# A cross network on one core: the residual's first tile turned by halves, a half store cut into two quarters around the last turn, and four sums done one by one

## The chip, the cores and the metric

The kernel runs on one core of one Trainium2 chip. The metric is the device time of one execution in microseconds (us); the medians and ranges below are over several runs. A profiled execution gives the rows that are quoted: start and duration of each instruction on TensorE (PE, and PEld for its weight loads), VectorE (DVE), ScalarE (ACT), GpSimd (POOL), and of the DMA issues on SyncE's and ScalarE's queues (SPq, ACTq).

## The reference

The input has B = 16384 rows of D = 416 features in bf16. Six layers follow, each with a 416 x 416 weight:

```python
x = x0
for l in range(L):                       # L = 6
    proj = jnp.einsum('bd,de->be', x, ws[l]) + bs[l]
    x = x0 * proj + x
return x                                 # (16384, 416), bf16
```

So each layer is a matmul, a bias, a product with the input and a sum with the layer's own input (the residual).

## The kernel before

**Tiles and jobs.** The rows are cut into eight groups of 2048, and a job (g, l) is layer l of group g. Inside a job everything is turned: features lie on the partitions, rows along the free axis, in four chunks of 512 rows (j = 0 to 3). The 416 features are three full tiles of 128 (i, or t, = 0 to 2) and a remainder of 32, whose four chunks are packed into one tile of 128 partitions (the "tail"). The 48 jobs run in the order of the list `order`, in which several groups are under way at once so that no job waits for the one before it. The last jobs are (7,4), (6,5) and (7,5): the eighth group is group 7, the seventh is group 6.

**From a chunk to the next layer.** For a tile of a job, TensorE adds up the products of a chunk in a PSUM bank. ScalarE evacuates it with the bias (line 567), VectorE multiplies two chunks at a time with x0 (line 579) and adds the job's input (line 584), which gives the next layer's x. From the job (0,2) on, TensorE's order is the string `ORDER`, which `replay` turns into a list of matmuls of 32 rows each; the function `evacuate_chunk` is called when a chunk is done, and after the sum of two chunks (a "half" of the tile) it calls what depends on it.

**Queues.** `add` appends an instruction to the queue of its engine, in program order, and notes what it reads and writes. `_solve` puts in the waits. All instructions of one engine's queue go in that order, so what is added to SP behind a waiting DMA waits too. A DMA belongs to a lane, a semaphore of its own. Within a lane, the DMAs of one batch wait until the batch before has landed; a batch is named by the argument of that name. At the end SP waits for every lane whose name starts with "out" (lines 163 and 181).

**The output of a group.** x is turned back by DMA transposes into `ost`, which has rows on the partitions, and stored. For group 6 this goes by halves: `half_done` issues the turn of a half tile as soon as its sum is there (line 921). After the turn of the second half of tile 1 it issues the store of the first half of the group's rows, 832 KB (`store(g, 0, 2)`, line 946). The halves of job (6,5) come in the order (0, first), (1, first), (2, first), (0, second), (1, second), (2, second), so the turn of the last one is the only turn behind that store. The remainder goes through `turn_rest` (line 916), its copy into `ost` through POOL (line 939). The store of the second half stands later in the program, behind the first tile store of group 7.

**The last job.** (7,5) is done the other way round: with the x as weights, so that the result has rows on the partitions and needs no turn. Its 2048 rows are four tiles kk of 512 rows, each in four parts j of 128 rows. For that, its residual has to be turned: `x5n`, in the space of the x0 of slot 5. `rest_turn` (line 958) does that by DMA for the tiles 0 and 1, and TensorE for tile 2 and the tail. Tile 0 is turned whole when it is finished, tile 1 by halves when it is finished. A memset on POOL (line 956), which writes the same tokens, stands for "the old x0 has been read". For each kk, ScalarE copies out the four parts (line 1206), VectorE multiplies them with x0 (`nat_mul`, line 1212) and adds the residual (`nat_add`, line 1218), and a store takes them out (`nat_store`, line 1225). For kk = 0 to 2 this goes in pairs of j, and one store takes all four (416 KB). For kk = 3 the products are single; the sums of j = 0 and 1 are one instruction, with one store of 208 KB, and those of j = 2 and 3 are single, with stores of 104 KB each, the first on SP, the second on ACT.

Of the kernel before, what the change touches and what calls it, by code (L numbers as in the profile page):

```python
# [3 lines left out]
P = 128  # L4
CH = 512
# [16 lines left out]
class Program:  # L22
# [12 lines left out]
    def add(self, eng, fn, reads=(), writes=(), lane=None, batch=None, hold=False, release=False, row=None):  # L35
        op = Op(eng, fn, lane, batch, row)
        deps = {}
        if eng == "pool":
            writes = list(writes) + ["pool"]
        for t in reads:  # L40
            w = self.writer.get(t)
            if w is not None:
                deps[id(w)] = (w, True)
        for t in writes:
            w = self.writer.get(t)
            if w is not None:
                deps[id(w)] = (w, True)
            for r in self.readers.get(t, ()):
                if id(r) not in deps:
                    deps[id(r)] = (r, False)  # L50
        for d, raw in deps.values():
            if d.lane is None and d.eng == eng and lane is None and (eng == "pe" or not raw):
                if row is None or d.row is None or row == d.row:
                    continue
            op.deps.append(d)
        for t in reads:
            self.readers.setdefault(t, []).append(op)
        for t in writes:
            self.writer[t] = op
            self.readers[t] = []  # L60
        if eng == "dve":
            if hold:
                self.flush()
                self.held = op
            else:
                self.queue[eng].append(op)
                if release:
                    self.flush()
        else:
            self.queue[eng].append(op)  # L70
        if lane is not None:
            batches = self.lanes.setdefault(lane, [])
            if not batches or batches[-1][0] != batch:
                batches.append((batch, []))
            batches[-1][1].append(op)
        return op
# [230 lines left out]
def bass_standalone__cross_network_dcn__recsys_kernel(  # L307
# [7 lines left out]
    L = ws.shape[0]  # L315
    NT = 3
    NJ = 4
    GC = NJ * CH
    NG = B // GC
    KK = CH // P  # L320
    assert D == NT * P + T32 and B == NG * GC and NG == 8 and L == 6
    LAST = NG - 1
# [26 lines left out]
    xs = [nc.alloc_sbuf_tensor(f"x_{s}", [P, XW], BF16) for s in range(NXS)]  # L349
# [205 lines left out]
    def evacuate_chunk(g, l, i, j, b, read):  # L555

        s0 = slot(g)
        if (g, l, i) not in tile_tw:
            tile_tw[(g, l, i)] = tw_n[0] % NTW
            tw_n[0] += 1  # L560
            tile_out[(g, l, i)] = set()
        r, out_ = tile_tw[(g, l, i)], tile_out[(g, l, i)]
        if (g, l + 1) not in xset:
            xset[(g, l + 1)] = free_x.pop(0)
        src, stok = x_src(g, l)
        so = xset[(g, l + 1)]
        add("act", lambda h: h.activation(  # L567
            tw[r][:, j * CH:(j + 1) * CH], bank(b), ACT_F.Identity, bias=bias[:, i, l:l + 1], scale=1.0),
            reads=[("ps", b), "bias"], writes=[("tw", r, j)])
        out_.add(j)  # L570
        a = j - j % 2
        ready[(g, l, i, a)] = max(ready.get((g, l, i, a), 0), read)
        if not {a, a + 1} <= out_:
            return
        both = (a, a + 1)
        o, c = slice(a * CH, (a + 2) * CH), slice(i * GC + a * CH, i * GC + (a + 2) * CH)

        def multiply():
            add("dve", lambda h: h.tensor_tensor(tw[r][:, o], tw[r][:, o], x0s[s0][:, c], ALU.mult),  # L579
                reads=[("tw", r, k) for k in both] + [x0_tok(s0, i, k) for k in both],  # L580
                writes=[("tw", r, k) for k in both], release=True)

        def plus():
            add("dve", lambda h: h.tensor_tensor(xs[so][:, c], tw[r][:, o], src(i, a, a + 2), ALU.add),  # L584
                reads=[("tw", r, k) for k in both] + [stok(i, k) for k in both],
                writes=[("x", so, i, k) for k in both], hold=True)
            if len(out_) == NJ or (g, l) in halved and i == NT - 1:
                pr.flush()

        todo = [multiply, plus]  # L590
        if (g, l) in halved:
            todo.append(lambda: half_done(g, l, i, a))
        if len(out_) == NJ:
            todo.append(lambda: finish_tile(g, l, 1, i))
        while todo:
            if behind_tail or phases and max(dve[0], ready[(g, l, i, a)]) + PAIR > phases[0] + 14:
                behind_tail.extend(todo)
                return
            step = todo.pop(0)
            if step in (multiply, plus):  # L600
                dve[0] = max(dve[0], ready[(g, l, i, a)]) + PAIR
            step()
# [316 lines left out]
    def turn_out(g, t, j0, j1):  # L919
        s = xset[(g, L)]  # L920
        add("sp", lambda h: h.dma_start_transpose(
            ost[:, j0 * KK:j1 * KK, t * P:(t + 1) * P], xs[s][:, t * GC + j0 * CH:t * GC + j1 * CH]),
            reads=[("x", s, t, j) for j in range(j0, j1)], writes=[("ost", t, j) for j in range(j0, j1)],
            lane=f"ot_{t}{j0}", batch=g)

    def half_done(g, l, i, a):
        turn_out(g, i, a, a + 2)
        if (i, a) == (NT - 2, 2):
            store(g, 0, 2)

    def spread(eng):

# [8 lines left out]
    def store(g, j0, j1):  # L941

        rows = out[g * GC + j0 * CH:g * GC + j1 * CH, :]
        o = ost[:, j0 * KK:j1 * KK, :].rearrange("p (j k) f -> p j k f", k=KK)
        pat = "(j p k) f -> p j k f" if g == 0 else "(j k p) f -> p j k f"
        add("sp", lambda h: h.dma_start(rows.rearrange(pat, j=j1 - j0, k=KK), o),
            reads=[("ost", t, j) for t in range(NT + 1) for j in range(j0, j1)],
            writes=[("out", g, j0)], lane="out", batch=(g, j0))

    x5f = x0s[s5][:, 0:XW + CH].rearrange("p (a f) -> p a f", f=D)  # L950

    def rest_turn(t):

        s = xset[(LAST, L - 1)]
        if t == 0:
            add("pool", lambda h: h.memset(warm[:, :], 0.0), writes=x0_all(s5) + x03_toks(s5) + ["x5 free"])
        for j0, j1 in ((0, NJ),) if t == 0 else ((0, 2), (2, NJ)):
            add("sp", lambda h, j0=j0, j1=j1: h.dma_start_transpose(
                x5f[:, j0 * KK:j1 * KK, t * P:(t + 1) * P], xs[s][:, t * GC + j0 * CH:t * GC + j1 * CH]),
                reads=[("x", s, t, j) for j in range(j0, j1)] + ["x5 free"],  # L960
                writes=[("x5n", j, t) for j in range(j0, j1)], lane=f"x5_{t}{j0}", batch=0)

    items = []
    where = {(b[0 if b in batches[4:-3] else min(1, len(b) - 1)], 0): b for b in batches[:-1]}
# [43 lines left out]
    def finish_tile(g, l, n=1, i=0):  # L1008
        tiles_done[(g, l)] = tiles_done.get((g, l), 0) + n
        if l == L - 1 and g == LAST - 2:  # L1010
            turn_out(g, i, 0, NJ)
        elif (g, l) == (LAST, L - 2) and i < NT - 1:
            rest_turn(i)
        elif (g, l, i) == (LAST - 1, L - 2, 0):
            spread("dve")
            store(LAST - 2, 0, NJ)
        if tiles_done[(g, l)] == NT:
            done_with(g, l)
# [190 lines left out]
    def nat_mul(kk, j, n=2):  # L1209
        o, x0v = on[:, j:j + n, kk, :], x0n7[:, j:j + n, kk, :]  # L1210
        toks = [("on", a, kk) for a in range(j, j + n)]
        add("dve", lambda h: h.tensor_tensor(o, o, x0v, ALU.mult),  # L1212
            reads=toks + [("n7", k) for k in range(KK)], writes=toks)

    def nat_add(kk, j, n=2):
        o, x5v = on[:, j:j + n, kk, :], x5n[:, j:j + n, kk, :]
        toks = [("on", a, kk) for a in range(j, j + n)]
        add("dve", lambda h: h.tensor_tensor(o, o, x5v, ALU.add),  # L1218
            reads=toks + [("x5n", a, t) for a in range(j, j + n) for t in range(NT + 1)], writes=toks)
# [33 lines left out]
    for kk in range(1, KK):  # L1253
        begun = (1,) if kk == 1 else ()
        nat_rows(kk, bks[kk], begun=begun)
        for j in range(NJ):
            nat_full(kk, j, bks[kk][j], False, (2,) if j in begun else range(NT))
            nat_out(kk, j, bks[kk])
            if kk == last:
                nat_mul(kk, j, 1)  # L1260
            elif j % 2:
                nat_mul(kk, j - 1)
                nat_add(kk, j - 1)
            if kk == last and j == 1:
                nat_add(kk, 0)
                nat_store(kk, 0, 2)
        if kk < last:
            nat_store(kk, 0, NJ)
# [33 lines left out]
```

## Time and profile before

| | |
|---|---|
| median of 3 runs | 466.54 us |
| lowest and highest | 466.38 and 467.29 us |
| profiled execution | 466.98 us |
| its span | 465.2 us |
| mean granted TensorE clock | 0.999 |
| busy: PE, DVE, ACT, POOL | 458.9, 403.3, 381.9, 7.2 us |
| moved by DMA | 53.78 MB, 116 GB/s in the mean |

The span runs from the first to the last instruction of the execution; the profiled execution's own time is 1.78 us longer. A row of the time line has the start, the duration, the engine or queue, the line of the kernel, the operation, what is written from what, the shape and the count. For a DMA on SPq or ACTq the duration is that of its issue by the queue, not of the transfer. A row of busy shares by stretch has the stretch and its length, then the busy time (and count) of PE, PEld, DVE, ACT and POOL, and last the granted clock, the mean busy share of the 16 DMA engines and what they moved in GB/s; the share can be a little over 1, since packets overlap.

### The profile page before, as it was taken

The page shows a single profiled execution, that of the slowest core. Times are in us where ns is not written, and L with a number is a line of the kernel's source. Part 1 is how long each engine was busy: PE and PEld are TensorE (multiplying, and loading weights), DVE is VectorE, ACT ScalarE, POOL GpSimd, SP SyncE. Part 2 cuts the span into 40 slices and gives each one's busy share as a digit, 9 for nine tenths or more (in the row PEclk, how much of TensorE's full clock was granted, in tenths as well). Part 3 has the DMA queues.
Part 4 walks back from the last instruction along what each step waited for, and adds up shares of the span by engine and source line. Part 5 has one row for each costly group of instructions (what it writes and reads, how often), then busy time and mean ns, then how long its engine had stood idle before and what let it go on. Part 6 is the DMA issues. An engine that isn't in the chain of part 4 may idle for free.

```text
span 465.2 us, 17826 instructions
## 1 busy us (share of the span) xinstructions
PE 458.9 (99%) x8001; PEld 267.2 (57%) x8001; DVE 403.3 (87%) x696; ACT 381.9 (82%) x609; POOL 7.2 (2%) x15
## 2 busy tenths in 40 slices
PE   9999999999999999999999999999999999999995
PEld 5444656575655556565665556566556665556552
DVE  1887888988889898898988979898988988989996
ACT  4686889887988889797888889888888887988884
POOL 1000000000000000000000000000000000000000
PEclk9999999999999999999999999999999999999999
DMA  8985759000002849086469616677100088182898
GB/s 228 188 174 127 166 118 195 13 23 9 19 4 36 157 163 194 14 133 179 91 136 130 182 29 92 96 121 216 26 2 4 25 148 296 38 137 65 200 162 291
DMA packets 136720, 53.78 MB, mean 116 GB/s; under 512 B 113210, under 2 KB 135236, under 8 KB 136644
## 3 DMA queue, kind: packets, MB, share of 16 engines
q1 hardware_dynamic: 136488, 52.54, 52.4%
q8 instruction: 62, 1.02, 0.9%
q10 hardware_dynamic: 156, 0.11, 0.1%
q14 instruction: 14, 0.11, 0.1%
HBM read 5.97 MB, written 13.63 MB: 42 GB/s over the span
## 4 chain that ended last, share of the span: by engine, by line
PE 94%; DVE 2%; DMA 1%; ACT 1%; SPq 1%; issue 0%; DVEq 0%
PE ps L1092 73%; PE ps L708 7%; PE ps L1096 6%; PE ps L661 4%; PE ps L655 1%; PE ps L696 1%; DMA x<-in_x_dram 1%; DVE x L1218 1%; DVE x L1212 1%; ACT tw L567 1%; PE ps L682 1%; SPq L751 0%; DVE tw L579 0%; DVE x L584 0%; PE ps L806 0%
## 5 line engine op out<-in xcount | busy, mean ns | idle before, releaser
L1092 PE MATMUL ps<-x,wm 32*128 32x512 bf16 x6288 | 372.8, 375 | 0.0
L567 ACT ACTIVATE tw<-ps,bias 128x512 bf16<-128x512 f32 x524 | 326.9, 688 | 48.8 <-PE ps L1092 35.9
L1092 PEld LDWEIGHTS ps<-x,wm 32*128 32x128 bf16 x6288 | 222.6, 92 | 134.7 <-ACT tw L567 6.4
L579 DVE TENSOR_TENSOR tw<-tw,x 128x1024 bf16<-128x1024 bf16 x262 | 177.1, 690 | 41.0 <-ACT tw L567 39.6
L584 DVE TENSOR_TENSOR x<-tw,x 128x1024 bf16<-128x1024 bf16 x262 | 171.2, 689 | 0.3
L1096 PE MATMUL ps<-x,w 32*128 32x512 bf16 x524 | 159.7, 375 | 0.0
L1096 PEld LDWEIGHTS ps<-x,w 32*128 32x128 bf16 x524 | 44.6, 92 | 5.9
L708 PE MATMUL ps<-x,wm 128*32 128x512 bf16 x564 | 33.6, 380 | 0.0
L628 ACT ACTIVATE ts<-ps,bias 128x512 bf16<-128x512 f32 x32 | 20.4, 685 | 13.1 <-PE ps L696 13.1
L531 ACT ACTIVATE tw<-ps,bias 128x1024 bf16<-128x1024 f32 (+1 forms) x24 | 20.7, 937 | 8.2 <-PE ps L682 7.0
L708 PEld LDWEIGHTS ps<-x,wm 128*32 128x32 bf16 x564 | 13.5, 96 | 18.2 <-ACT tw L567 3.7
L661 PE MATMUL ps<-x,wm 128*128 128x512 bf16 x92 | 21.6, 384 | 0.0
L632 DVE TENSOR_TENSOR x<-ts,x 128x512 bf16<-128x512 bf16 x47 | 18.4, 420 | 0.3
L661 PEld LDWEIGHTS ps<-x,wm 128*128 128x128 bf16 x92 | 8.5, 98 | 11.5 <-issue 2.3
L540 DVE TENSOR_TENSOR tw<-tw,x 128x1024 bf16<-128x1024 bf16 (+1 forms) x21 | 13.1, 637 | 2.2 <-ACT tw L531 2.1
L624 DVE SCALAR_TENSOR_TENSOR ts<-ps,bias,x 128x512 bf16<-128x512 f32 x15 | 11.2, 747 | 3.1 <-PE ps L696 3.1
L545 DVE TENSOR_TENSOR x<-tw,x 128x1024 bf16<-128x1024 bf16 (+1 forms) x21 | 12.6, 635 | 0.0
L630 DVE TENSOR_TENSOR ts<-ts,x 128x512 bf16<-128x512 bf16 x32 | 12.4, 418 | 0.0
L939 POOL COPY ost<-ot 128x512 bf16<-128x512 bf16 x6 | 5.8, 964 | 390.4 <-DMA ot<-x 390.4
L816 DVE COPY x<-ps 128x512 bf16<-128x512 bf16 x5 | 2.0, 423 | 8.7 <-PE ps L806 8.7
L1157 PE MATMUL ps<-wm,x 128*128 128x416 bf16 x48 | 9.3, 340 | 0.0
L1206 ACT ACTIVATE x<-ps 128x416 bf16<-128x416 f32 x16 | 7.7, 528 | 1.5 <-PE ps L1157 1.5
(51 smaller groups left out, 72.9 us busy)
## 6 DMA issues: line engine op xcount, KB each, us to landing
out_dram<-ost SPq DMA_DIRECT2D x6, 1664.0 KB, 7.7
x<-x SPq DMA_DIRECT2D x24, 96.0 KB, 2.2
x<-in_x_dram SPq DMA_DIRECT2D x8, 208.0 KB, 3.9
x<-in_x_dram SPq DMA_DIRECT2D x4, 416.0 KB, 8.0
out_dram<-ost SPq DMA_DIRECT2D x2, 832.0 KB, 4.2
wm<-in_ws_dram SPq DMA_DIRECT2D x5, 312.0 KB, 3.4
x<-x SPq DMA_DIRECT2D x22, 64.0 KB, 2.0
out_dram<-x SPq DMA_DIRECT2D x3, 416.0 KB, 4.5
```

The costliest lines, as they stand in the source:

```text
L531: add("act", lambda h, a=a, w=w, b0=b0: h.activation(tw[r][:, a * CH:(a + w) * CH], psum[:, b0 * CH:(b0 + w) * CH], ACT_F.Identity, bias=b ...
L540: add("dve", lambda h, a=a, e=e: h.tensor_tensor(tw[r][:, a * CH:e * CH], tw[r][:, a * CH:e * CH], x0s[s0][:, i * GC + a * CH:i * GC + e * ...
L545: add("dve", lambda h, a=a, e=e: h.tensor_tensor(xs[so][:, i * GC + a * CH:i * GC + e * CH], tw[r][:, a * CH:e * CH], src(i, a, e), ALU.ad ...
L567: add("act", lambda h: h.activation(tw[r][:, j * CH:(j + 1) * CH], bank(b), ACT_F.Identity, bias=bias[:, i, l:l + 1], scale=1.0), reads=[( ...
L579: add("dve", lambda h: h.tensor_tensor(tw[r][:, o], tw[r][:, o], x0s[s0][:, c], ALU.mult), reads=[("tw", r, k) for k in both] + [x0_tok(s0 ...
L584: add("dve", lambda h: h.tensor_tensor(xs[so][:, c], tw[r][:, o], src(i, a, a + 2), ALU.add), reads=[("tw", r, k) for k in both] + [stok(i ...
L628: add("act", lambda h: h.activation(ts[r][:, :], bank(b), ACT_F.Identity, bias=bias[:, 3, l:l + 1], scale=1.0), reads=[("ps", b), "bias"], ...
L632: add("dve", lambda h: h.tensor_tensor(x3s[so][:, :], ts[r][:, :], res, ALU.add), reads=[("ts", r)] + rtok, writes=[("x3", so), ("x3", so, ...
L661: add("pe", lambda h, t=t, j=j: h.matmul(bank(banks[j]), wm[l][:, t, ecols], src(t, j, j + 1), start=(first and t == 0), stop=(not first a ...
L708: add("pe", lambda h, t=t, j=j, src=src, l=l, b=b, ro=ro, qo=qo: h.matmul(psum[qo, b * CH:(b + 1) * CH], wm[l][:, t, NT * P:D], src(t, j, ...
L1092: add("pe", lambda h, l=l, t=t, j=j, b=b, q=q, ecols=ecols, src=src, kw=kw: h.matmul(bank(b), wm[l][q, t, ecols], src(t, j, j + 1)[q, :], ...
L1096: add("pe", lambda h, l=l, b=b, q=q, ecols=ecols, s3=s3, kw=kw: h.matmul(bank(b), w3[l][q, ecols], s3[q, :], **kw), reads=tok3 + [("w3", l ...
```

## The change

Three places are changed.

1. The residual of the last job: tile 0 of job (7,4) is turned by halves, each behind its own sum, through the same hook that group 6's last job uses. Tile 1 stays by halves, issued when the tile is finished. `rest_turn` now does one half per call, and the memset on POOL goes with the first call.
2. The seventh group's first half store (832 KB) becomes two quarter stores (416 KB each). The first is issued just ahead of the last turn, the second just behind it. Each start j0 of a store has a lane of its own (`out0`, `out1`, `out2`) in place of the one lane `out`, so the second half store no longer waits for the first to land.
3. In the last tile (kk = 3) the sums of j = 0 and j = 1 are two instructions, each behind its product, in place of one of twice the size behind both products.

```diff
         todo = [multiply, plus]
-        if (g, l) in halved:
+        if (g, l) in halved or (g, l, i) == (LAST, L - 2, 0):
             todo.append(lambda: half_done(g, l, i, a))
...
     def half_done(g, l, i, a):
+        if g == LAST:
+            rest_turn(i, a)
+            return
+        if (i, a) == (NT - 1, 2):
+            store(g, 0, 1)
         turn_out(g, i, a, a + 2)
-        if (i, a) == (NT - 2, 2):
-            store(g, 0, 2)
+        if (i, a) == (NT - 1, 2):
+            store(g, 1, 2)
...
-            writes=[("out", g, j0)], lane="out", batch=(g, j0))
+            writes=[("out", g, j0)], lane=f"out{j0}", batch=g)
...
-    def rest_turn(t):
+    x5_free = []
+
+    def rest_turn(t, j0):
 
         s = xset[(LAST, L - 1)]
-        if t == 0:
+        if not x5_free:
+            x5_free.append(True)
             add("pool", lambda h: h.memset(warm[:, :], 0.0), writes=x0_all(s5) + x03_toks(s5) + ["x5 free"])
-        for j0, j1 in ((0, NJ),) if t == 0 else ((0, 2), (2, NJ)):
-            add("sp", lambda h, j0=j0, j1=j1: h.dma_start_transpose(
-                x5f[:, j0 * KK:j1 * KK, t * P:(t + 1) * P], xs[s][:, t * GC + j0 * CH:t * GC + j1 * CH]),
-                reads=[("x", s, t, j) for j in range(j0, j1)] + ["x5 free"],
-                writes=[("x5n", j, t) for j in range(j0, j1)], lane=f"x5_{t}{j0}", batch=0)
+        j1 = j0 + 2
+        add("sp", lambda h: h.dma_start_transpose(
+            x5f[:, j0 * KK:j1 * KK, t * P:(t + 1) * P], xs[s][:, t * GC + j0 * CH:t * GC + j1 * CH]),
+            reads=[("x", s, t, j) for j in range(j0, j1)] + ["x5 free"],
+            writes=[("x5n", j, t) for j in range(j0, j1)], lane=f"x5_{t}{j0}", batch=0)
...
-        elif (g, l) == (LAST, L - 2) and i < NT - 1:
-            rest_turn(i)
+        elif (g, l, i) == (LAST, L - 2, 1):
+            rest_turn(i, 0)
+            rest_turn(i, 2)
...
             if kk == last:
                 nat_mul(kk, j, 1)
+                if j < 2:
+                    nat_add(kk, j, 1)
...
             if kk == last and j == 1:
-                nat_add(kk, 0)
                 nat_store(kk, 0, 2)
```

## The prediction

> **What bounds the kernel now.** I read four views in this order: the chain of work that ended last, the busy shares by stretch of the last 16 us, the time line of SP's queue, and the time line of VectorE. All times are us from the start of the span. The page's chain by engine:
>
> ```profile
> PE 94%; DVE 2%; DMA 1%; ACT 1%; SPq 1%; issue 0%; DVEq 0%
> ```
>
> Up to about 459.7 TensorE sets the time, and no part of the change takes a matmul away. So only the piece behind TensorE, and the queues that feed it, can move the end. The busy shares by stretch (length, five engines, TensorE clock, mean share of the 16 DMA engines, GB/s):
>
> ```profile
> 449.75:457.50 7.75, 7.75 (x71) 3.92 (x70) 7.61 (x15) 6.83 (x15) 0.00 (x0) 1.00 1.09 276
> 457.50:458.50 1.00, 1.00 (x7) 0.53 (x8) 0.96 (x3) 0.42 (x2) 0.00 (x0) 1.00 0.27 98
> 458.50:464.00 5.50, 1.20 (x7) 0.47 (x5) 2.84 (x8) 1.72 (x4) 0.00 (x0) 0.99 1.05 374
> 464.00:465.20 1.20, 0.00 (x0) 0.00 (x0) 0.00 (x0) 0.00 (x0) 0.00 (x0) 0.50 0.08 24
> ...
> 457.75:458.00 0.25, 0.25 (x4) 0.14 (x2) 0.25 (x2) 0.00 (x0) 0.00 (x0) 1.00 0.00 0
> 458.00:458.25 0.25, 0.25 (x3) 0.15 (x2) 0.25 (x1) 0.10 (x1) 0.00 (x0) 1.00 0.00 0
> ```
>
> The DMA engines are full from 449.75 to 464.1 (1.2 x 0.08 = 0.1 us past 464.00) but for one hole. In the stretch 457.50 to 458.50 the share is 0.27 where the neighbours have 1.05, so 1 - 0.27/1.05 = 0.74 us is lost. The five compute engines are done at 461.4; the last 2.7 us are DMA backlog. So the end of this kernel is: when the stores have been moved. SP's queue shows what makes the hole:
>
> ```profile
> 450.16 1.33 SPq L921 DMA_TRANSPOSE ost<-x  x1
> 451.65 0.46 SPq L946 DMA_DIRECT2D out_dram<-ost  x1
> 452.16 2.13 SPq L921 DMA_TRANSPOSE ost<-x  x1
> 454.47 1.27 SPq L1225 DMA_DIRECT2D out_dram<-x  x1
> 457.43 0.37 SPq L946 DMA_DIRECT2D out_dram<-ost  x1
> 457.85 0.58 SPq L1225 DMA_DIRECT2D out_dram<-x  x1
> 460.26 0.72 SPq L1225 DMA_DIRECT2D out_dram<-x  x1
> 461.12 1.10 SPq L1225 DMA_DIRECT2D out_dram<-x  x1
> 461.40 0.38 ACTq L1225 DMA_DIRECT2D out_dram<-x  x1
> ...
> SPq L168 <- DMA ost<-x: 1.6, 1, 1.6
> ...
> DMA to landing us min/median/max: 3.2/4.5/5.5
> ```
>
> The seventh group's second half store (457.43) reads what the last turn (452.16) writes. SP is through with the tile store before it at 454.47 + 1.27 = 455.74 and then waits 1.6 us for that turn to land, about 457.35, inside the landings of 3.2 to 5.5 us after issue that line 921 shows. Its first packets follow some 0.9 us later, at about 458.35 (the share is 0.00 up to 458.25), when all that was queued is gone: that is the hole. The tile store of 457.85 stands behind the same wait although its sum was ready at 456.70 (below).
>
> **The stores around the last turn.** The turn lands late because 832 KB of store stand ahead of it:
>
> ```profile
> 452.50:455.25 2.75, 2.75 (x21) 1.23 (x22) 2.71 (x6) 2.43 (x5) 0.00 (x0) 1.00 1.07 319
> 455.25:456.50 1.25, 1.25 (x9) 0.69 (x7) 1.22 (x3) 1.01 (x2) 0.00 (x0) 1.00 1.19 234
> ...
> 451.15 0.69 DVE L584 TENSOR_TENSOR x<-tw,x 128x1024 bf16<-128x1024 bf16 x1
> 453.36 1.09 DVE L1218 TENSOR_TENSOR x<-x,x 128x832 bf16<-128x832 bf16 x2
> 456.11 0.59 DVE L1218 TENSOR_TENSOR x<-x,x 128x832 bf16<-128x832 bf16 x1
> ```
>
> From 452.50 to 455.25 the engines move 319 GB/s, nearly all of it the half store (0.85 MB, 2.6 us); the fall to 234 GB/s after it is the turn with its small packets. In the change only a quarter (0.43 MB, 1.3 us) stands ahead. It is issued at the same place, about 451.65: on SP nothing lies between the old place (after the turn of 450.16) and the new one (before the turn of 452.16), and the turns whose output it reads are the ones the half store read. The turn is issued at about 452.1 (its sum is ready at 451.15 + 0.69 = 451.84) and lands 1.3 us earlier, at 456.0. The second quarter does not read the last turn; SP issues it when the turn's issue is over, at 453.4 (1.26 us, the shortest half turn) to 454.3 (2.13 again), and the first tile store behind it at 454.5 to 454.7 (sum ready at 454.45). The second half store can then go at about 456.1; with 0.9 us its packets come at 457.0, before the engines run dry at 457.6, as the bytes ahead are the same ones in another order. Margin 0.6 us. The hole closes: **-0.74**. Bounds: 0 if the turn lands no earlier, -0.74 if it closes wholly. I take the upper one, since even a turn issue of 2.13 and a store issue of 1.27 leave SP free by 456.0. Behind it the next limit is the sums: the tile store behind the half store is ready at 456.70, ahead of its bytes' turn.
>
> The lanes: the half store of 457.43 also waited for the first half store to land; that had landed before the turn behind it (SP's one wait there is put down to the turn), so dropping it is worth 0. What it costs is two more lanes to wait for at the end, on SP behind landed stores: 0 to 2 x 0.04 (0.04 is the gap between two SP issues that wait for nothing, 444.98 + 1.34 to 446.36, below). I take **+0.08**.
>
> **The rule against it.** The Trainium skill, "Perfetto Trace Analysis", section DMA Optimizations, says that splitting DMAs can let work start and finish sooner if the engines are generally idle. Here they are at 1.05 to 1.09, so by that rule the split buys nothing and the sum is +0.1; the trace's answer is the one hole, which the rule's average does not see. The skill's "DMA: Bandwidth & Descriptors", section Bandwidth, asks for transfers of 1 MiB and more, and the quarter is 416 KB. The trace does not agree here: the share stays at 1.05 from 458.50 to 464.00, across stores of 832, 416, 208 and 104 KB.
>
> **Residual's first tile by halves.** SP's queue and the two sums of that tile:
>
> ```profile
> 434.90 0.68 DVE L584 TENSOR_TENSOR x<-tw,x 128x1024 bf16<-128x1024 bf16 x1
> 435.50 0.69 DVE L584 TENSOR_TENSOR x<-tw,x 128x1024 bf16<-128x1024 bf16 x1
> ...
> 436.22 1.73 SPq L958 DMA_TRANSPOSE x<-x  x1
> 438.34 1.57 SPq L958 DMA_TRANSPOSE x<-x  x1
> 439.95 1.51 SPq L958 DMA_TRANSPOSE x<-x  x1
> 441.51 2.07 SPq L916 DMA_TRANSPOSE ot<-x  x1
> 443.68 1.26 SPq L921 DMA_TRANSPOSE ost<-x  x1
> 444.98 1.34 SPq L921 DMA_TRANSPOSE ost<-x  x1
> 447.85 2.27 SPq L921 DMA_TRANSPOSE ost<-x  x1
> ...
> 448.50:449.00 0.50, 0.50 (x5) 0.27 (x4) 0.39 (x1) 0.50 (x2) 0.00 (x0) 1.00 0.01 1
> ```
>
> Before, one turn of 1.73 starts when the second sum is there (436.19). Now a half starts at 435.6 and the other behind it. At 1.34 each they end at 438.3, about when the second tile's first half starts anyway (438.34, where SP had waited 0.39 from 437.95); at 1.57 each they end at 438.8, so 0.5 later. What follows on SP is a row of issues with hardly a gap, to 452.16, so a shift at 438 can travel. On the other side: the DMA engines start 0.6 us sooner, and the second tile's halves, now 1.57 and 1.51 behind a full turn, would cost 1.34 or 1.26 with less in front: 0.40 to 0.56 earlier at the turn of 441.51. That one (2.07) and the one of 447.85 (2.27) sit in stalls of the DMA engines (share 0.01 at 448.50), which swallow part of any shift either way. Bounds at the last turn +0.5 and -0.5; the nearest rows are the half turns one behind another (1.26, 1.34), so I take **-0.2**. The result itself is read after 453; the memset on POOL that it hangs on has long run. Nothing waits for it.
>
> **The sums of the last tiles.** VectorE:
>
> ```profile
> 458.88 0.37 DVE L1212 TENSOR_TENSOR x<-x,x 128x416 bf16<-128x416 bf16 x1
> 459.23 0.38 DVE L1212 TENSOR_TENSOR x<-x,x 128x416 bf16<-128x416 bf16 x1
> 459.64 0.59 DVE L1218 TENSOR_TENSOR x<-x,x 128x832 bf16<-128x832 bf16 x1
> 460.15 0.37 DVE L1212 TENSOR_TENSOR x<-x,x 128x416 bf16<-128x416 bf16 x1
> 460.44 0.37 DVE L1212 TENSOR_TENSOR x<-x,x 128x416 bf16<-128x416 bf16 x1
> 461.01 0.37 DVE L1218 TENSOR_TENSOR x<-x,x 128x416 bf16<-128x416 bf16 x1
> ```
>
> One sum of 832 (0.51 to the next start) becomes two of 416 (0.29 each, from 460.15 to 460.44), and each waits for the product before it: a product followed by its own sum takes 0.41 (459.23 to 459.64). So product, sum, product, sum is 0.41 + 0.29 + 0.41 + 0.29 = 1.40 against 458.88 to 460.15 = 1.27 now: all behind it comes 0.13 later, the store of the first two tiles at 460.39, the last on ACT at 461.53. Cover: the DMA backlog. Before, the last issue (461.40) plus 0.9 us could have moved at 462.3, while the engines were busy to 464.1; after, 462.4, busy to 463.2. Cost **0**, and 0.13 if the backlog were gone. This is also the floor: 461.53 + 0.9 + 0.6 (0.21 MB of the last two stores at 374 GB/s) = 463.0, so no gain beyond 1.1 us.
>
> **Sum.** -0.74 + 0.08 - 0.2 + 0 = -0.86. The profiled execution took 466.98 (465.2 of span and 1.78 around it), so 466.1; it lies 0.44 above the median of the runs, 466.54, from which I forecast **465.7**.
>
> **The rivals.**
> - *The turn lands no earlier, or splitting has a fee.* If the turn's landing hangs on its own issue (2.13) rather than on the bytes ahead, or if the added transfer pays its 0.9 us start uncovered, the hole stays. For it: 1.27 for the issue at 454.47 shows SP held up too. Against it: the engines never pause between the transfers they have. This is also where the two rules above lead. 466.54 + 0.08 = 466.6. Chance 0.12.
> - *The row on SP gains all it can.* The turns run 0.5 earlier up to 452.16, which is then tied to its sum at 451.84 (0.3 earlier), and the backlog shrinks to its floor: -1.1 to -1.2, 465.4. For it: every half turn before 450 is issued later than SP would without the one ahead. Against: the two stalls. Chance 0.15.
> - *The added half turn makes the row late.* If both halves of the first tile fall into a stall (2.27 each, as at 447.85), the second tile starts at 435.6 + 4.6 = 440.2 in place of 438.34, 1.9 later, and the row carries it to the last turn: -0.74 + 0.08 + 1.9 = +1.2, 467.8, slower. It decides from a delay of 0.66 on at the turn of 441.51. Against: no stall shows on SP between 436 and 439. Chance 0.12.
>
> **How the numbers follow.** The forecast has 0.61. A measurement of this kernel tells about 0.2% (0.93 us) from no change, and the forecast of -0.86 sits just inside; by its bounds for the row on SP (0 to -0.5) about half lies on either side: 0.31 faster, 0.30 the same. With the rivals: faster 0.31 + 0.15 = 0.46; same 0.30 + 0.12 = 0.42; slower 0.12. The likeliest alone spans 465.3 to 466.0. The range goes from the floor with 0.2 of measurement, 465.2, to 466.8, above the first rival, and leaves out the slow rival and a little of the fast one.
>
> **What would show it.** Right: the share of the DMA engines near 1 from 457.5 to 458.5; the second half store issued near 456.1; the wait on the turn under 0.5 us; the row of turns on SP no later than before at 441.51 and 450.16; the first two last tiles stored near 460.4. Wrong: the hole kept or moved; the turn of 441.51 later; the last store alone with idle engines ahead of it.

## The result, and the profile after

The changed kernel takes 465.44 us in the median of 10 runs (464.80 to 466.08), the one before 466.39 in 10 runs beside them. The ratio is 0.9978 with a 95% interval of 0.9969 to 0.9988, so the change gains 0.6 to 1.4 us, and 0.95 by the medians. Forecast were 465.7 and a gain of 0.86. The profiled execution took 465.16 us, with a span of 463.4 us.

The busy shares by stretch of the changed kernel (columns as in the prediction: stretch, length, PE, PEld, DVE, ACT, POOL, clock, DMA share, GB/s):

```profile
449.25:457.00 7.75, 7.75 (x71) 3.86 (x69) 7.61 (x15) 6.83 (x16) 0.00 (x0) 1.00 1.09 296
457.00:458.00 1.00, 1.00 (x10) 0.60 (x7) 0.97 (x3) 0.42 (x2) 0.00 (x0) 1.00 1.07 346
458.00:461.50 3.50, 1.30 (x8) 0.49 (x6) 3.03 (x9) 1.82 (x4) 0.00 (x0) 1.00 1.02 385
461.50:462.50 1.00, 0.00 (x0) 0.00 (x0) 0.00 (x0) 0.00 (x0) 0.00 (x0) 0.92 0.66 218
462.50:463.40 0.90, 0.00 (x0) 0.00 (x0) 0.00 (x0) 0.00 (x0) 0.00 (x0) 0.50 0.00 0
```

The hole is gone: 1.07 where the kernel before had 0.27. By the shares the engines' work ends at 462.2 or so (0.66 of the stretch from 461.50); before it was 464.1. SP's queue of the changed kernel, and its wait for the last turn:

```profile
440.66 1.91 SPq L916 DMA_TRANSPOSE ot<-x  x1
448.91 1.31 SPq L921 DMA_TRANSPOSE ost<-x  x1
450.39 0.46 SPq L951 DMA_DIRECT2D out_dram<-ost  x1
451.47 1.29 SPq L921 DMA_TRANSPOSE ost<-x  x1
452.80 0.58 SPq L951 DMA_DIRECT2D out_dram<-ost  x1
454.07 0.35 SPq L1234 DMA_DIRECT2D out_dram<-x  x1
454.68 0.37 SPq L951 DMA_DIRECT2D out_dram<-ost  x1
456.33 0.35 SPq L1234 DMA_DIRECT2D out_dram<-x  x1
460.84 0.33 SPq L1234 DMA_DIRECT2D out_dram<-x  x1
461.13 0.39 ACTq L1234 DMA_DIRECT2D out_dram<-x  x1
...
SPq L168 <- DMA ost<-x: 0.2, 1, 0.2
...
DMA to landing us min/median/max: 3.1/4.1/5.5
```

The last turn (451.47) lands 3.1 us after its issue, the least of line 921, where it took 5.2 before. The second half store waits 0.2 us for it in place of 1.6 and goes at 454.68 in place of 457.43. The turn's own issue takes 1.29 in place of 2.13, and the store issues behind it 0.33 to 0.58 in place of up to 1.27.

One caution in comparing two profiles. ScalarE's last copy marks the end of the matmuls:

```profile
459.74 0.52 ACT L1206 ACTIVATE x<-ps 128x416 bf16<-128x416 f32 x1
```

and in the changed kernel

```profile
459.34 0.52 ACT L1215 ACTIVATE x<-ps 128x416 bf16<-128x416 f32 x1
```

That is 0.40 us earlier, and VectorE, ScalarE and TensorE already have this lead at 28 us, long before anything that was changed: it comes from the start of that one execution. So I compare the stretch from that copy to the end of the span, which is 465.18 and 463.36 us to the hundredth: 465.18 - 459.74 = 5.4 us before, 463.36 - 459.34 = 4.0 after.

### The profile page after: what moved, and what is told of

It is laid out like the page before. It is cut to its first block, busy times and chain, and to the rows that moved or that the text cites. A ratio compares the mean times of both kernels' runs of the same rounds, so it can differ in the third digit from the quotient of the medians.

```text
span 463.4 us, 17830 instructions
## 1 busy us (share of the span) xinstructions
PE 458.5 (99%) x8001; PEld 266.8 (58%) x8001; DVE 403.5 (87%) x697; ACT 381.9 (82%) x609; POOL 7.7 (2%) x15
## 4 chain that ended last, share of the span: by engine, by line
PE 95%; DVE 4%; issue 0%; ACT 0%; DVEq 0%
PE ps L1101 73%; PE ps L708 7%; PE ps L1105 6%; PE ps L661 4%; PE ps L655 1%; PE ps L696 1%; DVE x L1227 1%; DVE x L584 1%; DVE x L1221 1%; DVE tw L579 1%; PE ps L806 1%; PE ps L788 1%; PE ps L682 1%; ACT tw L567 0%; DVE x L1189 0%
```

## The experiments

Each run was compared with the kernel before in runs beside it on the same chip (medians of before 466.39 to 467.01 from one set of runs to the next). "To the end" is the stretch just named, from each run's own profile. The kernel before against itself (e12) gives a ratio of 0.9989 with 1 inside the interval, so a ratio near 0.999 tells little alone, and what is worth half a microsecond or less is read from the profiles.

| run | what it is | median us | ratio to before (95%) | to the end, us |
|---|---|---|---|---|
| before | | 466.39 | 1 | 5.4 |
| e12 | before, again | 466.58 | 0.9989 (0.9973 to 1.0005) | 5.0 |
| full change | | 465.44 | 0.9978 (0.9969 to 0.9988) | 4.0 |
| e7 | full change, again | 465.78 | 0.9980 (0.9971 to 0.9989) | 4.0 |
| e1 | residual's halves alone | 466.35 | 0.9996 (0.9987 to 1.0006) | 4.6 |
| e2 | quarter stores alone | 466.29 | 0.9990 (0.9981 to 1.0000) | 4.9 |
| e3 | single sums alone | 466.63 | 0.9997 (0.9986 to 1.0009) | 5.0 |
| e4 | halves and quarters | 465.36 | 0.9972 (0.9960 to 0.9984) | 4.3 |
| e11 | the same, again | 465.52 | 0.9981 (0.9972 to 0.9990) | 4.0 |
| e5 | full, both quarters ahead of the turn | 466.12 | 0.9989 (0.9980 to 0.9997) | 4.8 |
| e6 | full, half store whole behind the turn | 466.68 | 1.0001 (0.9992 to 1.0009) | 5.3 |
| e8 | e4, one sum left out | 465.87 | 0.9982 (0.9973 to 0.9991) | 4.6 |
| e9 | full, second residual tile whole | 465.55 | 0.9981 (0.9972 to 0.9989) | 4.0 |
| e10 | e9 with the paired sum | 465.26 | 0.9976 (0.9966 to 0.9987) | 4.0 |

**The three parts one by one.** e1 keeps only the edit of the residual:

```diff
-        elif (g, l) == (LAST, L - 2) and i < NT - 1:
-            rest_turn(i)
+        elif (g, l, i) == (LAST, L - 2, 1):
+            rest_turn(i, 0)
+            rest_turn(i, 2)
```

(with the hook for tile 0 as in the change).

> Only the residual's first tile by halves; the 832 KB half store, the one lane and the paired sum stay as before. Theory (both the row of turns on SP and the order of the stores give): the row of turns runs 0.4 to 0.9 us earlier from the turn of the remainder on, the half store's bytes and the last turn behind them move with it, the second half store goes some 1 us earlier than 457.4 (less what TensorE runs early or late), and the time falls by 0.5 to 1.2 us against before. Rival (only the stores around the last turn count, the residual is read late and nothing waits for it): within 0.2 us of before.

Its profile, the shares from 456.00 on, then the two SP rows that matter:

```profile
456.00:456.25 0.25, 0.25 (x3) 0.06 (x1) 0.25 (x2) 0.25 (x1) 0.00 (x0) 1.00 0.96 386
456.25:456.50 0.25, 0.25 (x6) 0.10 (x8) 0.25 (x1) 0.25 (x1) 0.00 (x0) 1.00 0.09 27
456.50:456.75 0.25, 0.25 (x8) 0.02 (x5) 0.22 (x2) 0.24 (x1) 0.00 (x0) 1.00 0.00 0
456.75:457.00 0.25, 0.25 (x8) 0.11 (x2) 0.25 (x1) 0.25 (x1) 0.00 (x0) 1.00 0.13 47
...
440.48 1.97 SPq L916 DMA_TRANSPOSE ot<-x  x1
...
451.32 2.00 SPq L921 DMA_TRANSPOSE ost<-x  x1
```

The row on SP is early: the remainder's turn stands 18.71 us ahead of the last copy (459.19 here), against 18.23 before (459.74 - 441.51). But the last turn still has 832 KB ahead (issue 2.00), and the hole is still there, some 0.7 us of it, only earlier. The time gains 0.2 us by the ratio, within an interval that holds zero. The expected 0.5 to 1.2 did not come out in the time. This one profile has 4.6 us to the end, 0.4 less than the second profile of before and 0.8 less than the first, but its execution was the shortest of the run's eleven.

e2 keeps only the stores and the lanes:

```diff
-        if (i, a) == (NT - 2, 2):
-            store(g, 0, 2)
+        if (i, a) == (NT - 1, 2):
+            store(g, 1, 2)
```

(with `store(g, 0, 1)` ahead of the turn, and the lanes by j0).

> Only the two quarter stores around the last turn and the lanes; residual and sums as before. Theory: the row of turns stands as before (41.51 and 50.16 past 400), the last turn lands some 1.3 us earlier after its issue, the hole of 0.74 us in the DMA engines closes, and the time falls by 0.5 to 0.8 us. Rival (the gain comes from the row on SP alone): within 0.2 us of before, the hole kept.

In e2's profile the place of the hole and the rows on SP:

```profile
457.50:457.75 0.25, 0.25 (x5) 0.15 (x3) 0.25 (x1) 0.10 (x1) 0.00 (x0) 1.00 0.89 320
457.75:458.00 0.25, 0.25 (x4) 0.12 (x2) 0.25 (x2) 0.00 (x0) 0.00 (x0) 1.00 1.03 346
...
441.56 2.13 SPq L916 DMA_TRANSPOSE ot<-x  x1
...
452.20 1.48 SPq L921 DMA_TRANSPOSE ost<-x  x1
...
456.02 0.37 SPq L948 DMA_DIRECT2D out_dram<-ost  x1
...
SPq L168 <- DMA ost<-x: 0.9, 1, 0.9
```

The row stands where it was, the hole is closed, the half store goes at 456.02: the prediction's rows nearly one for one (456.1). The wait on the turn is still 0.9 us, but the engines have enough queued to cover it. The ratio gives 0.5 us (0 to 0.9), where 0.74 was the price.

e3 keeps only the sums.

```diff
                 nat_mul(kk, j, 1)
+                if j < 2:
+                    nat_add(kk, j, 1)
```

> Only the two single sums in the last tile. Theory: VectorE's last sum ends 0.12 us later, the DMA backlog of 2.7 us behind it covers that, time within 0.15 us of before. Rival (the sums are what made the change faster): 0.3 us or more faster than before.

No difference that this run can tell: its interval reaches half a microsecond either way, and the price was 0.13. Its profile shows the cover, since the DMA engines stay full to the end of the transfers:

```profile
462.00:463.00 1.00, 0.00 (x0) 0.00 (x0) 0.00 (x0) 0.00 (x0) 0.00 (x0) 0.50 1.00 364
```

e4 leaves this part out of the full change:

> The residual's halves and the quarter stores, with the sum of the first two parts of the last tile paired as before. Theory: with the backlog gone the end hangs on VectorE's last sum, so without the extra instruction this is 0.1 to 0.15 us faster than the full change, 1.05 to 1.2 us under before; the last store's issue on ACT is 0.12 us earlier against TensorE's last matmul. Rival (the end is still the DMA backlog): the same as the full change, 0.95 under before.

Together the two parts give 1.3 us by the ratio and, in the second run (e11), 0.9. The full change gave 1.0 and, again, 0.9. So the sums neither help nor cost anything that these runs can tell, and the expected 0.1 for leaving them paired cannot be read from them. What these runs do tell is that the stores count: e4 and e1, measured side by side, differ in the stores and their lanes alone, and their intervals (0.9960 to 0.9984 and 0.9987 to 1.0006) lie apart, if barely (e11's reaches 0.9990).

> The full change once more, on the chip of these runs. All theories: 0.7 to 1.2 us under before; the profile shows no hole from 457 to 459 and the residual's row on SP some 0.4 us early at the remainder's turn.

> The residual's halves and the quarter stores with paired sums, a second time, beside the two others. Theory: 1.0 to 1.3 us under before; against the full change the paired sum is worth 0.1 us or nothing, which these runs can hardly tell.

**Split or place?** e5 splits the store, but leaves both quarters where the half stood:

```diff
         if (i, a) == (NT - 1, 2):
             store(g, 0, 1)
+            store(g, 1, 2)
         turn_out(g, i, a, a + 2)
-        if (i, a) == (NT - 1, 2):
-            store(g, 1, 2)
```

> The full change, but both quarter stores ahead of the last turn: split, in the old place. Theory (what stands ahead of the turn counts): the turn lands some 1.3 us later after its issue than in the full change (4.4 to 5.2 us in place of 3.1), a hole of about 0.6 us in the DMA engines comes back ahead of the second half store, and the time is that of the residual's halves alone, 0 to 0.4 us under before. Rival (the split itself or the free lanes give it): as the full change, 0.95 us under before, no hole.

```profile
457.00:457.25 0.25, 0.25 (x9) 0.08 (x8) 0.22 (x1) 0.24 (x2) 0.00 (x0) 1.00 0.46 173
457.25:457.50 0.25, 0.25 (x9) 0.08 (x2) 0.25 (x1) 0.25 (x1) 0.00 (x0) 1.00 0.00 0
457.50:457.75 0.25, 0.25 (x2) 0.13 (x3) 0.25 (x1) 0.09 (x1) 0.00 (x0) 1.00 0.06 20
...
SPq L168 <- DMA ost<-x: 1.5, 1, 1.5
```

The hole and the wait of 1.5 us are back, and with 4.8 us to the end most of the profile's gain is gone. In the time e5 is 0.5 us under before, the full change in the runs beside it (e7) 0.9; those two intervals overlap, so the loss rests on the profile. The free lanes are in e5 too, and did not prevent it. e6 puts the whole half store behind the turn:

```diff
-        if (i, a) == (NT - 1, 2):
-            store(g, 0, 1)
         turn_out(g, i, a, a + 2)
         if (i, a) == (NT - 1, 2):
-            store(g, 1, 2)
+            store(g, 0, 2)
```

> The full change, but the first half store whole and behind the last turn: unsplit, nothing ahead of the turn. Theory: the turn lands early (3 to 3.3 us after its issue) and no hole is left ahead of the second half store, but the DMA engines run dry ahead of the turn, whose sum is only ready then (about 1.2 us of a hole, from the end of the turn before to its first packets), so the backlog is back at the end: 0.3 us under before to 0.2 over it. Rival (only the early landing counts): as the full change, 0.95 under, or faster.

```profile
452.00:452.25 0.25, 0.25 (x6) 0.14 (x3) 0.25 (x2) 0.25 (x1) 0.00 (x0) 1.00 0.38 73
452.25:452.50 0.25, 0.25 (x3) 0.17 (x2) 0.25 (x2) 0.25 (x1) 0.00 (x0) 1.00 0.00 0
452.50:452.75 0.25, 0.25 (x4) 0.10 (x2) 0.25 (x2) 0.25 (x1) 0.00 (x0) 1.00 0.17 37
...
SPq L168 <- DMA ost<-x: 0.2, 1, 0.2
```

Now the second half store waits only 0.2 us for its turn, as in the full change, and yet the kernel is no faster than before: the engines run dry ahead of the turn instead, 0.6 us here (half of what was expected, and about as much as the old hole), and the bytes that could have gone in that hole come at the end. So it is neither the split nor the early landing alone. Of the three amounts tried ahead of the last turn, none, one quarter and two, one quarter fills the time until the turn's packets are there without holding its landing up.

**What bounds the end now?** e8 leaves out the sum of the first two parts of the last tile, half a microsecond of VectorE's work:

```diff
             if kk == last and j == 1:
-                nat_add(kk, 0)
                 nat_store(kk, 0, 2)
```

> The residual's halves and the quarter stores with paired sums, but the sum of the first two parts of the last tile left out (these rows lack the residual), so VectorE's last sums end 0.5 us earlier. Theory (VectorE's last sum and the last store's own latency are the bound once the backlog is gone): 0.3 to 0.5 us faster than the same kernel with that sum, that is 1.6 to 1.8 us under before. Rival (the DMA engines' bytes are still the bound): within 0.15 us of it, 1.2 to 1.35 under before.

It gains nothing that shows: 465.87 us, against 465.78 for the full change in the runs beside it (e7). But its edit does not do what was expected of it. The products wait for ScalarE's copies, so VectorE's last sum starts at 460.57, 1.13 us behind the start of the last copy (459.44); in e11, which has the sum in question, it is 460.50 - 459.24 = 1.26. That is 0.13 us earlier and not 0.5, too little for these runs. In its profile the engines go on as before:

```profile
458.00:462.50 4.50, 1.41 (x9) 0.59 (x6) 2.60 (x8) 1.93 (x4) 0.00 (x0) 1.00 1.04 379
462.50:463.00 0.50, 0.00 (x0) 0.00 (x0) 0.00 (x0) 0.00 (x0) 0.00 (x0) 1.00 0.35 117
...
460.57 0.37 DVE L1227 TENSOR_TENSOR x<-x,x 128x416 bf16<-128x416 bf16 x1
460.97 0.38 ACTq L1234 DMA_DIRECT2D out_dram<-x  x1
...
DMA to landing us min/median/max: 2.5/3.4/4.8
```

The last issue is at 460.97, and its bytes have to wait their turn (2.5 us at least to land, 1.7 in the full change). But this execution had more bytes left at the end: its second half store went 3.7 us behind the issue of the last turn (451.57 to 455.29), in the full change 3.2 (451.47 to 454.68). So e8 does not decide between its two theories. Fine slices of the full change say more:

```profile
461.25:461.50 0.25, 0.00 (x0) 0.00 (x0) 0.00 (x0) 0.00 (x0) 0.00 (x0) 1.00 0.81 306
461.50:461.75 0.25, 0.00 (x0) 0.00 (x0) 0.00 (x0) 0.00 (x0) 0.00 (x0) 1.00 0.27 87
461.75:462.00 0.25, 0.00 (x0) 0.00 (x0) 0.00 (x0) 0.00 (x0) 0.00 (x0) 1.00 1.02 326
```

Here the engines have moved what was queued and run dry for some 0.2 us, until the last two stores (issued at 460.84 and 461.13) bring the share back. e7 has the same hole (0.33 in the slice from 462.00), e11 a smaller one (0.49 in the slice from 461.25). So in the profiles of the full change the end hangs on the last stores, and by them on VectorE's last sums. The bytes ahead are done only 0.2 us before, and in the profiles of e4 and e8, which have no such hole, the end is still the bytes. e9 tries to move SP's row still earlier, with one issue in place of two:

```diff
-            rest_turn(i, 0)
-            rest_turn(i, 2)
+            rest_turn(i, 0, NJ)
```

> The full change, but the residual's second tile turned whole in one issue, as its first tile was before. Theory (the row of issues on SP ahead of group 6's turns is what the residual's edit shortens, and each issue costs about 1 us whatever its size): one issue of some 1.75 us in place of two of 1.3, started 0.6 us later, so the remainder's turn is issued 0.3 us earlier than in the full change and the time falls by 0.1 to 0.4 us more, to 1.0 to 1.3 under before. Rival (the stall of the DMA engines just behind it swallows it): the turns of group 6 start as in the full change, time the same as it, 0.8 to 0.95 under before.

> As the run before, with the sum of the last tile's first two parts paired as before. Theory (the backlog is gone, the end hangs on VectorE's last sum and the last store): 0.1 to 0.15 us faster than with the single sums. Rival (the DMA engines' bytes are the bound): the same.

```profile
438.48 1.93 SPq L965 DMA_TRANSPOSE x<-x  x1
440.45 2.26 SPq L916 DMA_TRANSPOSE ot<-x  x1
```

The remainder's turn starts 0.14 us earlier against the end of the matmuls than in the full change, but takes 2.26 in place of 1.91 and ends 0.2 later: the stall swallows it. Further on there was little to gain for the turns: in the full change the last one already goes as soon as its sum is there (450.75 + 0.69 = 451.44 for the sum, 451.47 for the issue), 7.87 us ahead of the last copy, and in e9 it goes 7.87 us ahead of it too. The time is that of the full change. e10's 465.26 is the lowest median of all, but its interval and those of the full change overlap almost wholly; no version was shown to beat it.

**The two profiles of before.**

> The kernel before, unchanged, for a second profile of its end. If the profiles and the medians are to agree on the gain of about 0.95 us, the stretch from TensorE's last matmul to the end of the span is nearer 5.4 us here than the 5.8 us of the first profile (the full change has 4.4 in two profiles). If it is 5.8 again, the first 440 us differ between the kernels by some 0.4 us on average, which no part of the change explains.

That text measures from the start of TensorE's last matmul, about 0.4 us ahead of the last copy; the measure of the table gives 0.4 less. In that measure the second profile has 5.0 us to the end, the 5.4 of the text, and e3, whose row and stores are those of before, has 5.0 too; the first, 5.4, is the longest of the three. So 1.0 of the difference of 1.4 between the profile of before in the prediction and that of the full change is the change, in line with the medians. Where the first differs shows on SP: its last turn is issued 7.58 us ahead of the last copy (459.74 - 452.16), that of the second 7.86 (458.99 - 451.13), with the same program. e2 has 7.56 and is to be held against the first: 5.4 to 4.9.

## Why the prediction was right

The place and the mechanism were right, and the time lies 0.3 us under the forecast, inside the range. 0.15 of that is no gain: the kernel before took 466.39 us in the runs beside it, where the forecast starts from 466.54. The total of the sum is borne out (0.95 against 0.86). Its terms one by one are less sure, since the times of e1 and e2 have intervals of about half a microsecond either way.

- *The hole.* Priced at -0.74. e2, which has this part alone, closes it and gains 0.5 (0 to 0.9). The reason given, the bytes ahead of the last turn, is shown by the profiles of e5 and of the full change: same split, same lanes, both quarters ahead, and the hole is back.
- *The turn's landing.* Forecast 3.9 us after the issue and the half store at 456.1. e2 has 456.02. With the early row on SP it became 3.1 us and 454.68: the first quarter was then issued 1.08 us ahead of the turn (450.39 and 451.47), in e2 0.50 (451.70 and 452.20), so more of it was moved when the turn came. The two parts help each other here, which the sum did not have; the runs don't settle whether the gains are more than additive (0.2 + 0.5 alone, 0.9 to 1.3 together, each with an interval of about half a microsecond either way).
- *The row on SP.* Taken at -0.2, bounds 0.5 either way. Alone it gives 0.2 (from 0.6 faster to 0.3 slower). The halves behind one another take 1.26 to 1.35, as the nearest rows had it, so the rival of a late row fell: the remainder's turn was early in every profile with this edit, by some 0.4 us. At the last turn, for which the term was worked out, the row gains 0.3 against the first profile of before and nothing against the second, since the turn waits for its sum. What comes earlier there is the store ahead of it.
- *The rival of a row that gains all it can.* Chance 0.15, 465.4 us. Its rows are the ones that came: the remainder's turn 0.45 earlier (18.68 us ahead of the last copy in place of 18.23), the last turn tied to its sum, the backlog gone. The time, 465.44, is nearer to it than to the forecast of 465.7, and the runs can't tell the two apart. That the middle figure of -0.2 came out as well as it did is in part luck.
- *The lanes.* The +0.08 doesn't show. From the landing of the last store to the end of the span it is some 0.5 us in the changed kernel (461.13 + 1.7 to 463.4) and as much in e1, which has the one lane (460.86 + 2.4 to 463.8).
- *The sums.* 0 under the cover of the backlog: e3's profile shows the cover. The changed kernel has VectorE's rows at the steps 0.41 and 0.29 that were forecast:

```profile
458.48 0.37 DVE L1221 TENSOR_TENSOR x<-x,x 128x416 bf16<-128x416 bf16 x1
458.88 0.38 DVE L1227 TENSOR_TENSOR x<-x,x 128x416 bf16<-128x416 bf16 x1
459.17 0.37 DVE L1221 TENSOR_TENSOR x<-x,x 128x416 bf16<-128x416 bf16 x1
459.58 0.38 DVE L1227 TENSOR_TENSOR x<-x,x 128x416 bf16<-128x416 bf16 x1
459.87 0.37 DVE L1221 TENSOR_TENSOR x<-x,x 128x416 bf16<-128x416 bf16 x1
```

- *The floor.* Worked out as the last issue at 461.53, 0.9 us to its packets and 0.6 for its bytes, 463.0. The full change has come down to it: its last issue is at 461.13, which with the lead of 0.40 is 461.53, and the engines stop between 462.2 and 462.5 by the shares (462.6 by that sum, less the lead). Ahead of it stands the short hole at 461.50, in small what the prediction named as a sign of being wrong: the last store with idle engines ahead of it. It is the price of the floor and not of the hole at 457.5, which stays closed. With the backlog gone the extra sum could cost its 0.13; the last issue does come later with single sums, 461.13 - 459.34 = 1.79 us behind the last copy, than with paired ones (e11, 460.90 - 459.24 = 1.66), but the profiles of both have 4.0 us to the end. What more could be gained from the bytes or from the sums alone stays open, as the two limits lie 0.2 us apart.
- *The rules against it.* The Trainium skill, "Perfetto Trace Analysis", section DMA Optimizations, ties the gain of a split to idle engines. e5 agrees with it in its way: the split by itself did not close the hole. What pays is the order around a wait, and the mean share (1.05 to 1.09) hides that wait.

## What to carry to other kernels

Where a store waits for a transfer that stands in the same queue, count the bytes ahead of that transfer: put ahead of it just what fills the time until its own packets are there, and the rest behind. Look for the hole in fine slices of the DMA share rather than in its mean, and when it is closed, read the last slices again to see whether bytes or the last issue set the end. For gains of a fifth of a percent, measure one profile's tail from a mark at the end of the matmuls, and take a second profile of the kernel before.

## What the runs showed of the hardware that was not expected

The stalls of the turns at 441.5 and 447.9 may not be the turns' own. In the kernel before, the second one in two stretches:

```profile
447.75:448.50 0.75, 0.75 (x10) 0.25 (x4) 0.73 (x2) 0.75 (x3) 0.00 (x0) 1.00 3.24 170
448.50:449.75 1.25, 1.25 (x12) 0.78 (x11) 1.14 (x2) 1.25 (x4) 0.00 (x0) 1.00 0.05 6
```

For 1.25 us the 16 engines move next to nothing, though turns are queued; a share of 3.24 means that packets begun before it stayed open through it. All fourteen profiles have two such quiet stretches, of a little over a microsecond each, in the last 25 us, and within the microsecond ahead of each a single packet of 16 KB on the instruction queue starts. The page counts 62 such packets in the whole run:

```profile
q8 instruction: 62, 1.02, 0.9%
```

That they cause the stalls is likely by their timing, but no run took one away. The stalls, whatever their cause, would explain why a shift of SP's row by some tenths of a microsecond ahead of them is partly lost, as in e9.

The second is how long one and the same half turn, the last one, takes: its issue by SP 1.23 us (e6, nothing ahead) to 2.13 us (before, 832 KB ahead), and its landing 3.1 to 5.2 us after the issue.
